# Last attention head: every tile transposed by DMA, half of one output product moved into the loop, and the first output loads split 16, 15 and 1 heads

## The chip, the cores and the metric

The kernel runs on one core of a Trainium2 chip. The metric is the device time of one execution in microseconds. The kernel before takes 1593.01 us, the median of three runs (1591.46 to 1596.07).

The engines named below are TensorE (PE; weight loads are listed as PEld), VectorE (DVE), ScalarE (ACT), GpSimd (POOL) and SyncE (SP), which here only issues DMAs. The DMAs that SP issues form one queue in program order: SP issues one, then waits for whatever the next one needs, then issues that. Each compute engine also runs its own instructions in program order.

## The reference

An adaptive layer norm block with attention over a cache, followed by a token mixer and an MLP:

```python
mod = (_silu(c) @ w_mod).reshape(c.shape[0], 6, 1, -1)
h = _layernorm(x) * (1 + ca) + sa
x = x + ga * _A_ref(h, A_k_cache, A_v_cache, A_wq, A_wo)
h = _layernorm(x) * (1 + cb) + sb
x = x + gb * _B_ref(h, B_w1, B_w2, B_w3, B_w4)

def _A_ref(x, k_cache, v_cache, wq, wo):      # Sq = 2048, D = 640, H = 32, Sk = 2048, Dh = 128
    q = (x @ wq) per head
    p = softmax(q @ k_cache^T * Dh ** -0.5)
    return (p @ v_cache, heads side by side) @ wo
```

`_B_ref` is layer norm, a product with w1, GELU, a shift of four groups of channels along the sequence, a product with w2, then layer norm, w3, GELU and w4. Inputs and output are bf16.

## The kernel before

**Tiles.** The 2048 queries are 16 tiles of 128 (`NQT`). Attention is a loop over 512 tiles (`NG` = 32 heads x 16 tiles), one step `s` for each, and 12 more steps that drain it (`PVD` = 8, `LAG` = 4). Below, "tile 3 of the last head" is step 496 + 3.

**One step.** For each half of the 2048 keys, PE writes scores to the two halves of `Sps` (`qk`, lines 294 and 15). DVE scales them into `negS` with a running minimum (line 584). POOL joins the two minima (594). ACT writes exp to the ring slot `Pb[s % 10]` (597). The probabilities must then be transposed, keys on the partitions, into `PTs[s % 10]`. PE multiplies them with V eight steps later (`pv`, line 307), ACT copies two tiles' results out (575), POOL divides by the row sum (455) and writes four tiles at a time to `o_scratch` in HBM (462).

**Two ways to transpose.** Of 16 tiles, 14 go through a DMA from the ring to the ring (`transpose`, line 230), in pairs where both neighbours go this way and singly otherwise. Tiles 3 and 10 (`PE_TILES`) go through PE instead: 16 transposes (`t_piece`, line 261) into the two PSUM banks `Oaug` and `QPp`, and a copy out of each (`t_evac`, by ACT, line 270, or by DVE, line 272). So a head has six pairs and two singles, tiles 2 and 11, in the DMA queue. The two banks are also used by the query projections of the next head (`q_piece`, line 245), of which the last head has none.

**The SP queue in a head.** Beside the transposes it holds the next head's K (line 213), wq (217) and V (222). In the last head these are absent. There, `load_ot` (505) begins to fetch attention outputs of the first two query tiles (a "pair", `pr` = 0, for all heads) from `o_scratch`, transposed, into `hTx`: heads 0 to 11 after tile 2, heads 12 to 23 after tile 9, heads 24 to 31 after the last tile. Behind these come `load_xt(0, 1)` (512), whose target covers the ring slots of the last tiles and which therefore waits until the last transpose has landed, and `load_ot(1)`, all 32 heads of query tiles 2 and 3, into `negS`.

**The wo product.** `a_pe(j)` (line 532) accumulates 32 heads for query tile j into one half of `Sps`, 640 columns as 512 + 128, two matmuls for a head. Tile 0 is done in parts: heads 0 to 11 at step 515, heads 12 to 23 at step 516, the rest after the loop. Tile 1 has heads 0 to 11 at step 518 and the rest after the loop. Tiles 2 to 15 follow whole. `a_s1` and `a_s2` (645 to 659) apply the gate, the residual and the second layer norm; then the mixer (`b_op` 707, `c_op` 772) and the MLP (`d_op` 787, `e_op` 836) follow.

The helper `Prog` (line 20) puts the waits in: every operation names what it reads and writes, and an engine waits on the last writer or the readers.

Of the kernel before, what the change touches and what calls it, by code (L numbers as in the profile page):

```python
# [8 lines left out]
BF16 = mybir.dt.bfloat16  # L9
F32 = mybir.dt.float32  # L10
# [113 lines left out]
def bass_adaLN_cond__mha_block_cached__mixer_s_mlp__prompt_kernel(  # L124
# [15 lines left out]
    NG = H * NQT  # L140
# [5 lines left out]
    with ExitStack() as es:  # L146
# [4 lines left out]
        mod_bc = sb("mod_bc", [128, 4 * D], F32)  # L151
        Sps = ps("Sps", [128, 2048], F32)
        PTp = ps("PTp", [128, 2048], BF16)
        Oaug = ps("Oaug", [128, 512], F32)
        QPp = ps("QPp", [128, 512], F32)
        QPb = QPp[:].bitcast(BF16)

        if True:
            with ExitStack() as es1:
# [44 lines left out]
                s_col = flat[:, CO + 7 * KT:CO + 8 * KT]  # L204
                assert CO + 8 * KT <= 2 * RP * SK and XO + NQT * D <= WO_ and WO_ + KT * 2 * D <= 10 * SK
                PO = PTp[:].bitcast(F32)
                JB = [Oaug[:, 0:512], QPp[:, 0:512]]
                JBb = [Oaug[:].bitcast(BF16), QPb]
                G = Prog(nc, es1, "a")

                def load_k(h):
# [11 lines left out]
                          ("v", hb), w=[("V", hb)])  # L223

                assert RP % 2 == 0 and NQT % 2 == 0
                is_pe = lambda g: g % NQT in PE_TILES

                def transpose(g, n):
                    b = g % RP
# [283 lines left out]
                        xt[:, 4 * c0:4 * c1], x2d[c0 * 512:c1 * 512, :].rearrange("(t p) d -> p t d", p=128)),  # L513
                        ("xt", c0), w=[("x1", t) for t in range(4 * c0, 4 * c1)] + ringk(XT0 + 4 * c0 * D, XT0 + 4 * c1 * D))

                OTC = [0, 12 * H // 32, 24 * H // 32, H]
                yn = [0]

                def ybank():
# [3 lines left out]
                def a_pe(j, b=None, parts=(0, 1, 2), hs=None):  # L523
                    if b is None:
                        b = ybank()
                    pr, z = divmod(j, 2)
                    h0, h1 = hs or (OTC[parts[0]], OTC[parts[-1] + 1])

                    def f(t):
                        for c0, cw in NC2:  # L530
                            for hh in range(h0, h1):
                                ins = t.matmul(YB[b][:, c0:c0 + cw], OTj[pr % 2][:, 2 * hh + z, :], wo[:, hh, c0:c0 + cw],  # L532
                                               start=(hh == 0), stop=(hh == H - 1))
                        return ins
                    G.op("tensor", f, r=[("OT", pr % 2, i) for i in parts] + ["wo"], w=[("S", b)])
                    return b

                YB = [Sps[:, 0:1024], Sps[:, 1024:2048]]
                LAG = 4
                for s in range(NG + PVD + LAG):  # L540
                    h, j = divmod(s, NQT)
                    g_ = s - PVD
                    evacs = []
                    if s <= 2:
                        for i in ((0,), (1, 2), range(3, len(MROW)))[s]:
                            mod_rows(i)
                    if s == 3:
                        G.op("gpsimd", lambda g: g.tensor_scalar(
                            out=mod_bc[:, 2 * D:3 * D], in0=mod_bc[:, 2 * D:3 * D], scalar1=1.0, scalar2=1.0, op0=ALU.add, op1=ALU.mult),
                            r=[("mod", i) for i in range(len(MROW))], w=["mod"])  # L550
                    for half in range(2):
                        if s < NG:
                            qk(s, half)
                        if half == 0 and s in (NG + PVD - 5, NG + PVD - 4):
                            b0 = a_pe(0, None if s == NG + PVD - 5 else b0, (s - NG - PVD + 5,))
                        if half == 0 and s == NG + PVD - 2:
                            b1 = a_pe(1, None, (0,))
                        if 0 <= g_ < NG:
                            pv(g_, half)
                        if s == 0 and half == 1:  # L560
                            q_head0(NQC - 1)
                        if h + 1 < H and 2 * j + half in QPIECE:
                            cc, q = QPIECE[2 * j + half]
                            q_piece(h + 1, cc, q)
                            if q == KT - 1:
                                evacs.append((q_evac, h + 1, cc))
                        for r in range(2):
                            g = s - 3 - r
                            if 0 <= g < NG and is_pe(g):
                                t_piece(g, r, half)  # L570
                                if half == 1:
                                    evacs.append((t_evac, g, r))
                    if 0 <= g_ < NG and g_ % 2 == 1:
                        p = g_ // 2
                        G.op("scalar", lambda a, p=p: a.copy(  # L575
                            Of[:, p % 4].rearrange("p z d -> p (z d)")[:, 0:259], PO[:, (p % 2) * 512:(p % 2) * 512 + 259]),
                            r=[("O", p % 2)], w=[("Of", p % 4)])
                    for fn, x, y in evacs:
                        if fn is q_evac or not by_dve(x, y):
                            fn(x, y)  # L580
                    for half in range(2):
                        if s < NG:
                            r8 = s % 8
                            G.op("vector", lambda v, half=half, s=s, r8=r8: v.tensor_scalar(  # L584
                                out=negS[:, s % 3, half * 1024:(half + 1) * 1024],
                                in0=Sps[:, half * 1024:(half + 1) * 1024],
                                scalar1=-SCALE, scalar2=None, op0=ALU.mult, op1=ALU.min,
                                accum_out=(nm0 if half == 0 else nm1)[:, r8:r8 + 1]),
                                r=[("S", half)], w=[("negS", s % 3), ("nmh", half, r8)])
                    for fn, x, y in evacs:  # L590
                        if fn is t_evac and by_dve(x, y):
                            fn(x, y)
                    if s < NG:
                        G.op("gpsimd", lambda g, r8=r8: g.tensor_scalar(  # L594
                            out=nm[:, r8:r8 + 1], in0=nm0[:, r8:r8 + 1], scalar1=nm1[:, r8:r8 + 1], scalar2=None, op0=ALU.min),
                            r=[("nmh", 0, r8), ("nmh", 1, r8)], w=[("nm", r8)])
                        G.op("scalar", lambda a, s=s, r8=r8: a.activation(  # L597
                            Pb[:, s % RP, :], negS[:, s % 3, :], ACT.Exp, bias=nm[:, r8:r8 + 1], scale=-1.0),
                            r=[("negS", s % 3), ("nm", r8)], w=[("Pb", s % RP)])
                        if not is_pe(s):  # L600
                            if s % 2 == 1 and not is_pe(s - 1):
                                transpose(s - 1, 2)
                            elif s % 2 == 1 or is_pe(s + 1):
                                transpose(s, 1)
                        if j == 2 and h >= 1 and h + 1 < H:
                            load_k(h + 1)
                        if h + 1 == H and j in (2, PVD + 1):
                            i = 0 if j == 2 else 1
                            load_ot(0, OTC[i], OTC[i + 1], i)
                        if j == 6 and h + 2 < H:  # L610
                            load_wq(h + 2)
                        if j == PVD + 1 and h + 1 < H:
                            load_v(h + 1)
                    if 0 <= s - PVD - LAG:
                        gr, z = divmod(s - PVD - LAG, 4)
                        if z == 0:
                            rcp(gr)
                        norm(gr, z)
                    if s == NG:
                        G.op("gpsimd", lambda g: g.memset(mhalf, -0.5), w=["mhalf"] + NEG)  # L620
                        load_ot(0, OTC[2], OTC[3], 2)
                        load_xt(0, 1)
                        load_ot(1)
                    if s == NG + 2:
                        load_xt(1, NQC)
# [16 lines left out]

                def a_s1(j, b):
                    u = j % 2
                    G.op("vector", lambda v: v.tensor_mul(out=tmp[:, u], in0=YB[b][:, 0:D], in1=mod_bc[:, 0:D]),  # L645
                         r=[("S", b), "mod"], w=[("tmp", u)] + (TMPK if j < 2 else []))
                    G.op("vector", lambda v: v.tensor_add(out=xt[:, j], in0=tmp[:, u], in1=xt[:, j]),
                         r=[("tmp", u)], w=[("x1", j)])
                    stats_of(0, j, xt[:, j], ("x1", j))
# [77 lines left out]

                for i in range(NQT):
                    if i < NQT - 2:
                        b = a_pe(0, b0, (2,)) if i == 0 else a_pe(1, b1, (1, 2)) if i == 1 else a_pe(i)  # L730
                        if i >= 3:
                            n_t(i - 3, i == 3)
                    if i == NQT - 3:
# [174 lines left out]
```

## Time and profile before

| what | us |
|---|---|
| median of three runs | 1593.01 |
| the profiled execution, its time | 1592.4 |
| its span in the trace | 1590.6 |
| PE busy in the span | 1477.4 |
| DVE busy | 1395.0 |
| ACT busy | 1295.8 |
| POOL busy | 622.0 |
| DMA share of the hardware queue, of 16 engines' span | 98.5% |

The 1.8 us between the profiled execution's time and its span lie outside the trace. Matmuls are pipelined, so a busy PE isn't PE at its peak. An `SPq` row is a DMA-issuing instruction: its duration is the time for which SP is held by the issue, and the data land some microseconds later. Idle time ahead of an instruction stands in brackets with what ended it.

### The profile page before, as it was taken

What the parts mean: (1) busy time and instruction counts of PE and PEld (TensorE: products, weight loads), DVE (VectorE), ACT (ScalarE), POOL (GpSimd) and SP (SyncE); (2) the same over time, 40 slices, a digit from 0 to 9 for tenths busy, and PEclk for the clock granted to TensorE, in tenths of its full rate; (3) what the DMA queues carried; (4) which work ended last, traced back from release to release, by engine and by line L of the source; (5) the groups of instructions that cost most, each with busy time, mean ns of one, the idle gap of its engine ahead of it and who ended that gap; (6) DMA issues with size and microseconds to landing.
All of it is one profiled execution on the core that took longest, in us unless ns stands there. A gap on an engine that the chain in (4) does not pass through costs nothing.

```text
span 1590.6 us, 33595 instructions
## 1 busy us (share of the span) xinstructions
PE 1477.4 (93%) x13976; PEld 916.9 (58%) x13207; DVE 1395.0 (88%) x2463; ACT 1295.8 (81%) x1145; POOL 622.0 (39%) x1396
## 2 busy tenths in 40 slices
PE   5899999999999999999999999999999889999999
PEld 3466655656565556665556565565656655555555
DVE  6999999999999999999999999999999646666435
ACT  4999999999999999999999999999999700036330
POOL 0244444444444444444444444444444523223100
PEclk9999999999999999999999999999999999999999
DMA  9999999999999999999999999999999997503000
GB/s 300 236 235 237 240 236 239 242 233 251 235 245 236 233 242 241 239 244 228 245 238 236 236 248 230 243 242 237 243 230 236 240 248 135 127 1 112 9 26 34
DMA packets 1167900, 333.53 MB, mean 210 GB/s; under 512 B 1148352, under 2 KB 1161728, under 8 KB 1167744
## 3 DMA queue, kind: packets, MB, share of 16 engines
q1 hardware_dynamic: 1161600, 314.59, 98.5%
q0 software_dynamic: 6144, 16.79, 3.7%
q8 instruction: 108, 1.77, 0.5%
q14 instruction: 48, 0.39, 0.1%
HBM read 43.48 MB, written 19.40 MB: 40 GB/s over the span
## 4 chain that ended last, share of the span: by engine, by line
DVE 34%; ACT 22%; PE 21%; DMA 13%; issue 9%; POOL 2%; SPq 0%; POOLq 0%; DVEq 0%
DVE negS L584 31%; ACT ring L597 18%; DMA ring<-ring 12%; PE Sps L532 8%; PE Sps L836 4%; ACT ring L270 2%; PE Oaug L787 2%; PE QPp L787 2%; PE Sps L772 1%; ACT kv L252 1%; ACT Of L575 1%; PE PTp L307 1%; DVE ring L272 1%; DMA negS<-o_scratch 1%; POOL small L594 1%
## 5 line engine op out<-in xcount | busy, mean ns | idle before, releaser
L584 DVE TENSOR_SCALAR_CACHE_REDUCE negS<-Sps 128x1024 f32<-128x1024 f32 x1024 | 1178.6, 1220 | 30.9 <-PE Sps L15 30.5
L597 ACT ACTIVATE ring<-negS,small 128x2048 bf16<-128x2048 f32 x512 | 1029.6, 2018 | 22.8 <-POOL small L594 20.7
L307 PEld LDWEIGHTS PTp<-kv,ring 128*128 128x128 bf16 x8192 | 550.7, 98 | 382.7 <-issue 112.9
L307 PE MATMUL PTp<-kv,ring 128*128 128x129 bf16 x8192 | 645.7, 220 | 49.0 <-DMA ring<-ring 48.6
L15 PE MATMUL Sps<-kv 128*128 128x512 bf16 x1024 | 387.9, 379 | 12.6 <-DVE negS L584 6.6
L594 POOL TENSOR_SCALAR small<-small 128x1 f32<-128x1 f32 x512 | 145.8, 285 | 631.5 <-DVE negS L584 631.5
L294 PE MATMUL Sps<-kv 128*128 128x512 bf16 x926 | 355.3, 384 | 21.9 <-DVE negS L584 10.8
L455 POOL TENSOR_SCALAR On<-Of,small 128x128 bf16<-128x128 f32 x512 | 190.0, 371 | 13.0
L294 PEld LDWEIGHTS Sps<-kv 128*128 128x128 bf16 x1024 | 98.3, 96 | 109.3 <-DVE negS L584 87.2
L448 POOL TENSOR_TENSOR small<-Of,small 128x4 f32<-128x4 f32 x128 | 133.1, 1040 | 9.2 <-ACT Of L575 9.2
L675 ACT COPY kv<-PTp 128x640 bf16<-128x640 bf16 x32 | 22.0, 692 | 127.7 <-PE PTp L672 127.6
L462 POOL DMA_DIRECT2D o_scratch<-On x128 | 103.1, 806 | 40.8 <-POOL On L455 37.2
L575 ACT COPY Of<-PTp 128x259 f32<-128x259 f32 x256 | 96.0, 375 | 14.3 <-PE PTp L307 14.3
L245 PE MATMUL Oaug<-hTx,kv 128*128 128x512 bf16 x264 | 100.4, 385 | 3.4 <-DVE hTx L404 3.4
L245 PE MATMUL QPp<-hTx,kv 128*128 128x512 bf16 x259 | 97.5, 381 | 2.4 <-ACT hTx L399 1.7
L584 DVE DVE_READ_ACCUMULATOR negS<-Sps 128x1 f32 x1024 | 84.9, 83 | 0.0
L631 POOL TENSOR_SCALAR negS<-negS 128x1 f32<-128x1 f32 x48 | 24.7, 514 | 138.5 <-DVE negS L640 138.3
L532 PE MATMUL Sps<-wo,negS 128*128 128x128 bf16 (+1 forms) x503 | 71.4, 300 | 4.5 <-DMA negS<-o_scratch 4.1
L532 PE MATMUL Sps<-wo,hTx 128*128 128x512 bf16 (+1 forms) x502 | 69.3, 297 | 0.5
L645 DVE TENSOR_TENSOR ring<-Sps,mod_bc 128x640 f32<-128x640 f32 x16 | 13.2, 825 | 62.1 <-PE Sps L532 40.7
L270 ACT COPY ring<-Oaug 128x1024 bf16<-128x1024 bf16 x64 | 65.4, 1022 | 0.0
L840 DVE TENSOR_TENSOR ring<-Sps,ring 128x640 f32<-128x640 f32 x15 | 12.4, 824 | 58.5 <-PE Sps L836 58.5
(91 smaller groups left out, 1043.4 us busy)
## 6 DMA issues: line engine op xcount, KB each, us to landing
kv<-in_A_v_cache_dram SPq DMA_DIRECT2D x32, 512.0 KB, 5.0
o_scratch<-On POOLq DMA_DIRECT2D x128, 128.0 KB, 3.8
kv<-in_A_wq_dram SPq DMA_DIRECT2D x32, 160.0 KB, 3.3
wo<-in_A_wo_dram SPq DMA_DIRECT2D x1, 5120.0 KB, 17.2
ring<-ring SPq DMA_TRANSPOSE x256, 7.0
ring<-in_A_x_dram SPq DMA_DIRECT2D x5, 640.0 KB, 7.0
ring<-in_w_mod_dram SPq DMA_DIRECT2D x1, 3200.0 KB, 13.3
out_dram<-wo SPq DMA_DIRECT2D x15, 160.0 KB, 1.8
```

Source lines behind the costliest of these rows:

```text
L15: return t.add_instruction(mybir.InstMatmult(name=t.bass.get_next_instruction_name(), ins=[t.lower_ap(rhs), t.lower_ap(lhsT)], outs=[t.low ...
L245: G.op("tensor", lambda t: t.matmul(JB[jb], wq[:, hb, q, :], hT[:, q, cc * 512:(cc + 1) * 512], start=(q == 0), stop=(q == KT - 1)), r=[(" ...
L294: ins = (t.matmul if c2 == 0 else partial(same_weights, t))(Sps[:, col:col + 512], QT[:, hb, j * 128:(j + 1) * 128], KTs[:, hb, col:col + ...
L307: ins = t.matmul(ob[:, 0:129], PTs[:, b, kt, :], Vaug[:, hb, kt, 0:129], start=(kt == 0), stop=(kt == NKT - 1))
L448: G.op("gpsimd", lambda g: g.tensor_tensor(out=rl[:, 4 * b:4 * b + 4], in0=Of[:].rearrange("p a z d -> p (a z) d")[:, 4 * b:4 * b + 4, 128 ...
L455: G.op("gpsimd", lambda g: g.tensor_scalar(out=On[:, b, z, :], in0=Of[:, 2 * b + z // 2, z % 2, 0:128], scalar1=rl[:, 4 * b + z:4 * b + z ...
L462: G.dma("gpsimd", lambda e: e.dma_start(o_scr[jj // 2:jj // 2 + 2, :, hh].rearrange("a p z d -> p a (z d)"), On[:, b].rearrange("p (a z) d ...
L532: ins = t.matmul(YB[b][:, c0:c0 + cw], OTj[pr % 2][:, 2 * hh + z, :], wo[:, hh, c0:c0 + cw], start=(hh == 0), stop=(hh == H - 1))
L575: G.op("scalar", lambda a, p=p: a.copy(Of[:, p % 4].rearrange("p z d -> p (z d)")[:, 0:259], PO[:, (p % 2) * 512:(p % 2) * 512 + 259]), r= ...
L584: G.op("vector", lambda v, half=half, s=s, r8=r8: v.tensor_scalar(out=negS[:, s % 3, half * 1024:(half + 1) * 1024], in0=Sps[:, half * 102 ...
L594: G.op("gpsimd", lambda g, r8=r8: g.tensor_scalar(out=nm[:, r8:r8 + 1], in0=nm0[:, r8:r8 + 1], scalar1=nm1[:, r8:r8 + 1], scalar2=None, op ...
L597: G.op("scalar", lambda a, s=s, r8=r8: a.activation(Pb[:, s % RP, :], negS[:, s % 3, :], ACT.Exp, bias=nm[:, r8:r8 + 1], scale=-1.0), r=[( ...
```

## The change

1. `is_pe` is false in the last head: its tiles 3 and 10 are transposed by DMA too, so the singles of tiles 2 and 11 become pairs.
2. `Oaug` and `QPp` become the two halves of one PSUM tensor `Jps`.
3. Tile 0's wo product accumulates in `Jps`. A new function `y0_pe` issues heads 0 to 15 one at a time in steps 501 to 511, each behind the scores of its half step, heads 16 to 30 in steps 512, 513 and 514, five each, and head 31 after the loop. `a_s1(0)` reads `Jps`.
4. Tile 1's wo product takes over the places of tile 0: heads 0 to 11 at step 515, 12 to 23 at 516, 24 to 30 at 518, head 31 after the loop.
5. `load_ot(0)` is cut into heads 0 to 15 (after tile 0's step, ahead of the pair of tiles 0 and 1), 16 to 30 (after tile 4's step, ahead of the pair of tiles 4 and 5) and head 31 (after the last tile).

```diff
-        Oaug = ps("Oaug", [128, 512], F32)
-        QPp = ps("QPp", [128, 512], F32)
-        QPb = QPp[:].bitcast(BF16)
+        Jps = ps("Jps", [128, 1024], F32)
...
-                JB = [Oaug[:, 0:512], QPp[:, 0:512]]
-                JBb = [Oaug[:].bitcast(BF16), QPb]
+                JB = [Jps[:, 0:512], Jps[:, 512:1024]]
+                JBb = [b.bitcast(BF16) for b in JB]
...
-                is_pe = lambda g: g % NQT in PE_TILES
+                is_pe = lambda g: g % NQT in PE_TILES and g < NG - NQT
...
-                OTC = [0, 12 * H // 32, 24 * H // 32, H]
+                OTC = [0, H // 2, H - 1, H]
...
+                def y0_pe(h0, h1, parts):
+                    def f(t):
+                        for c0, cw in NC2:
+                            for hh in range(h0, h1):
+                                ins = t.matmul(Jps[:, c0:c0 + cw], OTj[0][:, 2 * hh, :], wo[:, hh, c0:c0 + cw],
+                                               start=(hh == 0), stop=(hh == H - 1))
+                        return ins
+                    G.op("tensor", f, r=[("OT", 0, i) for i in parts] + ["wo"], w=[("J", 0), ("J", 1)])
+
+                W1 = [OTC[1] + (OTC[2] - OTC[1]) * i // 3 for i in range(4)]
+                Y0 = {}
+                u = NG - NQT + 5
+                for hh in range(OTC[1]):
+                    if hh % 3 == 0 and hh:
+                        u += 2
+                    Y0[(u + hh % 3 // 2, hh % 3 % 2) if hh % 3 < 2 else (u + 1, 0)] = (hh, hh + 1, (0,))
+                for i in range(3):
+                    Y0[(NG + i, 0)] = (W1[i], W1[i + 1], (1,))
...
-                        if half == 0 and s in (NG + PVD - 5, NG + PVD - 4):
-                            b0 = a_pe(0, None if s == NG + PVD - 5 else b0, (s - NG - PVD + 5,))
+                        if (s, half) in Y0:
+                            y0_pe(*Y0[s, half])
+                        if half == 0 and s == NG + PVD - 5:
+                            b1 = a_pe(1, None, (0,), (0, 12 * H // 32))
+                        if half == 0 and s == NG + PVD - 4:
+                            b1 = a_pe(1, b1, (0, 1), (12 * H // 32, 24 * H // 32))
                         if half == 0 and s == NG + PVD - 2:
-                            b1 = a_pe(1, None, (0,))
+                            b1 = a_pe(1, b1, (1,), (24 * H // 32, OTC[2]))
...
-                        if h + 1 == H and j in (2, PVD + 1):
-                            i = 0 if j == 2 else 1
+                        if h + 1 == H and j in (0, 4):
+                            i = 0 if j == 0 else 1
                             load_ot(0, OTC[i], OTC[i + 1], i)
...
-                    G.op("vector", lambda v: v.tensor_mul(out=tmp[:, u], in0=YB[b][:, 0:D], in1=mod_bc[:, 0:D]),
-                         r=[("S", b), "mod"], w=[("tmp", u)] + (TMPK if j < 2 else []))
+                    G.op("vector", lambda v: v.tensor_mul(out=tmp[:, u], in0=(YB[b] if j else Jps)[:, 0:D], in1=mod_bc[:, 0:D]),
+                         r=([("S", b)] if j else [("J", 0), ("J", 1)]) + ["mod"], w=[("tmp", u)] + (TMPK if j < 2 else []))
...
-                        b = a_pe(0, b0, (2,)) if i == 0 else a_pe(1, b1, (1, 2)) if i == 1 else a_pe(i)
+                        b = y0_pe(OTC[2], H, (2,)) if i == 0 else a_pe(1, b1, (2,)) if i == 1 else a_pe(i)
```

## The prediction

> **What bounds the kernel now.** I read the page first, for the engines and the DMA share, then the chain around the end of the loop, then the SP queue and ACT in order of time there, and last PE behind it. The page, parts 1 to 3:
>
> ```profile
> PE 1477.4 (93%) x13976; PEld 916.9 (58%) x13207; DVE 1395.0 (88%) x2463; ACT 1295.8 (81%) x1145; POOL 622.0 (39%) x1396
> DMA  9999999999999999999999999999999997503000
> q1 hardware_dynamic: 1161600, 314.59, 98.5%
> ```
>
> Four resources are nearly full, and DMA is full in every slice up to about 1310 us. The averages don't say which one sets the end of the loop. The chain of waits there, 1255 to 1310 us:
>
> ```profile
> 1259.15 1.86 ACT ring L597
> 1261.01 5.90 DMA ring<-ring
> ...
> 1268.31 7.50 DMA ring<-ring
> ...
> 1275.82 0.42 DMA ring<-in_A_x_dram
> 1276.25 13.54 DMA negS<-o_scratch
> 1289.79 0.45 issue
> 1290.23 9.79 PE Sps L532 x63
> ```
>
> PE starts query tile 2 of the wo product at 1290.23, when `load_ot(1)` has landed. The PE row of that moment carries its wait, and the stages behind it are full of PE (columns: stretch, length, PE, PEld, DVE, ACT, POOL busy, clock, DMA share, GB/s):
>
> ```profile
> 1290.23 18.49 PE L532 MATMUL Sps<-wo,negS 128*128 128x512 bf16 x126 [4.12 <-DMA negS<-o_scratch]
> 1310.00:1400.00 90.00, 89.47 (x683) 51.95 (x692) 59.79 (x111) 7.46 (x11) 29.06 (x42) 1.00 0.60 119
> 1400.00:1500.00 100.00, 99.03 (x645) 52.72 (x655) 58.87 (x119) 53.01 (x86) 25.65 (x48) 1.00 0.13 45
> ```
>
> So the end is 1290.23 plus some 300 us of PE work that the change leaves as it is. Tiles 0 and 1 of the wo product were already done 4.12 us earlier. The question is only when `load_ot(1)` lands. The SP queue ahead of it (start, time SP is held):
>
> ```profile
> 1233.12 7.08 SPq L230 DMA_TRANSPOSE ring<-ring  x2
> 1240.25 3.56 SPq L505 DMA_TRANSPOSE hTx<-o_scratch  x1
> 1243.85 13.49 SPq L230 DMA_TRANSPOSE ring<-ring  x3
> 1257.38 3.58 SPq L505 DMA_TRANSPOSE hTx<-o_scratch  x1
> 1261.01 11.65 SPq L230 DMA_TRANSPOSE ring<-ring  x3
> 1272.78 2.70 SPq L505 DMA_TRANSPOSE hTx<-o_scratch  x1
> 1275.82 0.38 SPq L512 DMA_DIRECT2D ring<-in_A_x_dram  x1
> 1276.25 11.56 SPq L505 DMA_TRANSPOSE negS<-o_scratch  x1
> ```
>
> The rows stand end to end; SP is never free. Its 8 transposes are the last head's: pair 0-1 and single 2; pairs 4-5, 6-7, 8-9; single 11 and pairs 12-13, 14-15. ACT in the same time, the last five exps (tiles 11 to 15) and the copies of tile 10 between them:
>
> ```profile
> 1250.86 2.00 ACT L597 ACTIVATE ring<-negS,small 128x2048 bf16<-128x2048 f32 x1
> 1253.17 2.00 ACT L597 ACTIVATE ring<-negS,small 128x2048 bf16<-128x2048 f32 x1 [0.30 <-POOL small L594]
> 1255.33 1.01 ACT L270 COPY ring<-Oaug 128x1024 bf16<-128x1024 bf16 x1
> 1256.24 2.01 ACT L597 ACTIVATE ring<-negS,small 128x2048 bf16<-128x2048 f32 x1
> 1258.14 1.01 ACT L270 COPY ring<-QPp 128x1024 bf16<-128x1024 bf16 x1
> 1259.03 2.02 ACT L597 ACTIVATE ring<-negS,small 128x2048 bf16<-128x2048 f32 x1
> 1261.19 2.02 ACT L597 ACTIVATE ring<-negS,small 128x2048 bf16<-128x2048 f32 x1
> ```
>
> Tile 11's exp ends at 1252.9 and its transpose is issued at 1261.01; tile 15's ends at 1263.2 and its pair goes at 1268.31. The queue is 5 to 8 us behind ACT. The chain's step from exp to DMA at 1261 is an inferred releaser; by the rows that transpose waited for SP, which was issuing heads 12 to 23. In the last head, work added to the DMA queue is paid for; work taken from ACT or PE is not.
>
> **The change part by part.**
>
> *Two more tiles in the queue (and the PE path gone).* PE loses 32 transposes (about 3.1 us), ACT three copies of 1.01, DVE one of 0.69: nothing, since the queue covers it. The queue gains two tiles, 2 x 0.52 MB. The single of tile 2 holds SP 2.71 us (part of the 7.08), that of tile 11 1.75. Six pairs hold it 7.08 - 2.71 + 13.49 + 11.65 - 1.75 = 27.76, 4.63 each. Two singles become pairs: 2 x 4.63 - 4.46 = +4.8. By tiles, 32.22 us for 14 is 2.30 each: +4.6. I take +4.6, the mean over more rows. Ends: +3.5 (two tiles at 1.75) and +6.5 (both pairs like the slowest here, 5.47).
>
> The Trainium skill (DMA: Bandwidth & Descriptors, Latency and other measured facts) gives DMA transposes 261 GB/s, and 350 to 400 where contiguous; the two tiles would then take 4.0 us, or 2.6 to 3.0, and by that estimate the sum below would be +5.4, or +4.0 to +4.4, which is within 0.3%, the absorbed rival's side. The rows move a 1.05 MB pair in 4.63 us, 227 GB/s, so the trace is below both.
>
> *Output loads 16, 15, 1.* 24 heads took 3.56 + 3.58 = 7.14 us, 0.30 each. 31 heads now stand ahead of the last transposes: 9.2, +2.1 (end +4.0, at the 0.36 a head of the 11.56 row). The last part shrinks from 2.70 to some 0.3, but SP doesn't get that back: `load_xt(0,1)` behind it waits for the last pair to land (1268.31 + 7.50 = 1275.81) and is issued at 1275.82. What comes back is that less data stand before `load_ot(1)`. That takes 13.54 to land; the four lone ones later take 11.3, 11.4, 10.3 and 9.9, mean 10.7, and the 0.64 MB of x at 239 GB/s make 2.7, or 13.4. The old part landed 1.6 us into it. So between 0 and 1.6 is returned; I take 0.8. The last pair may land sooner with little behind it (landings of the last head's transposes run from 5.2 to 8.5 us; 7.5 now): I take 0.3, ends 0 and 0.8.
>
> *Wo heads in the loop.* 12 heads took 3.42 us, 0.28 a head. With 1.45 heads a step, PE has 4 score matmuls (about 0.22 apart), 16 of PV (1.12) and 0.41: 2.41 against DVE's 2 x 1.14 = 2.29. The first piece stands behind the first scores of step 501, which were at 1232.8. It needs heads 0 to 15, now issued at 1233.12 for 4.75 us and landed some 2.6 behind that, 1240.5. PE, and through it DVE and ACT, stops for 7 us. PV and the second scores of that step stand behind. Exp of step 501 then ends about 1245.5 and that of 511 ten steps of 2.41 later, 1269.6. The queue reaches its pairs at 1251.4 (4.75 + two pairs + 4.45 from 1233.12) and 1274: it never runs dry, with over 4 us to spare. I take 0. Without that cover each us lost is an us at the end.
>
> *PE behind the loop.* From step 512, about 1267.5: 8 tiles of PV 9.0, 15 + 31 heads 12.9, two heads 0.6: done at 1290. The 28 heads taken away behind the loop (7.55 us) gain nothing: PE waits for `load_ot(1)` anyway.
>
> *Clock.* PE idled 4.12 us before 1290.23; the stretch 1290.2 to 1300.1 had a clock of 0.88, and its tile took 9.79 against 8.64 later: 1.15 lost. The idle time is now about 5.5. Loss between 0.7 and 2.4: I take +0.4, ends -0.5 and +1.3.
>
> The Trainium skill (TensorE: Matmul & The Clock Gate, What's actually happening) says that a free-running window of 3.4 us idle halves the clock and a busy one restores it, so that the loss depends on where the window falls; the drop to 0.88 after 4.12 us fits.
>
> *Sum:* 4.6 + 2.1 - 0.8 - 0.3 + 0.4 = **+6.0**. `load_ot(1)` lands at 1295.4. On the profiled execution (span 1590.6, 1592.4 with the 1.8 outside it) that is 1598.4. It lies 0.6 below the median of the runs, so against 1593.01 I say 1599.0, 0.38% slower.
>
> **The rivals.**
>
> *The queue absorbs it (no change).* If the added tiles cost the queue less (the 1.75 row) and the smaller part ahead of `load_ot(1)` gives all of its 1.6 back, the landing moves by 3.5 + 2.1 - 1.6 - 0.8 = 3.2 and the clock may give 0.5: +2.7, 1595.7. It could go down to PE's own 1290 plus the 0.3 of the last issue, 1593. For it: no K, wq or V in this head. Against: SP isn't free for a moment in it.
>
> *The loop runs dry.* If step 501 resumes over 4 us later than reckoned, or PE's steps take 2.8, the last exps come after the queue: +3 more, 1602. For it: nothing in the trace before has PE wait for an output load in the loop. Against: the 4 us to spare.
>
> *Faster.* The chain of waits is right and the exps, not the queue, set the last transposes. Then three ACT copies (3.0) go, the short last part returns 2.4 of SP, and PE, not stopped at 501, is ready at 1282: `load_ot(1)` lands 5 earlier, 1588. It decides as soon as SP waits for an exp in the last head. Against: 5 to 8 us of lag in the rows.
>
> **How the numbers follow.** Forecast 0.64, absorbed 0.14, dry 0.12, faster 0.10. About 0.3% (4.8 us, so 1597.8) is what a measurement of this kernel can tell from no change. The forecast's own range is 1595.5 (low ends) to 1603.5 (4.0 for the loads, 6.5 for the tiles, part of the rest), and 0.10 of its 0.64 lies under 1597.8. Slower: 0.54 + 0.12 = 0.66; same: 0.10 + 0.14 = 0.24; faster 0.10. The range 1592.5 to 1604.5 leaves out the faster case and the worst of the dry one, under 0.2.
>
> **What would show it.** Right: in the SP queue eight pairs end to end, the last ending near 1279; `load_ot(1)` issued near 1282 and landing near 1295; PE idle about 5 us before tile 2; a PE wait of some 7 us at the first `y0_pe`. Wrong: gaps in the SP queue inside the last head (dry), transposes issued right at the end of their exps (faster), or tile 2 starting before 1293 (absorbed).

## The result, and the profile after

The changed kernel takes 1600.03 us against 1593.91 for the kernel before, both medians of 17 runs of each. The ratio is 1.0042 with a 95% interval of 1.0030 to 1.0054, that is 6.7 us slower (4.8 to 8.6). The forecast was 1599.0, 0.38% slower.

The page of the changed kernel, parts 1 to 3, shows no engine in trouble. PE and ACT have the same shares as before and DVE 87% against 88%, and the hardware queue moved 1.04 MB more, which is the two tiles:

```profile
PE 1494.7 (93%) x14199; PEld 916.0 (57%) x13175; DVE 1394.1 (87%) x2462; ACT 1294.5 (81%) x1142; POOL 625.2 (39%) x1396
DMA  9999999999999999999999999999999995603000
q1 hardware_dynamic: 1165696, 315.63, 97.9%
```

The SP queue of the changed kernel, from the last head's first entry (start, time SP is held). The lines of the loads, the transposes and the wo product are two lower than in the kernel before; those of the loop's scaling and exp, which stand behind `y0_pe`, are 20 higher:

```profile
1234.57 4.65 SPq L503 DMA_TRANSPOSE hTx<-o_scratch  x1
1239.26 9.78 SPq L228 DMA_TRANSPOSE ring<-ring  x2
1249.16 4.57 SPq L503 DMA_TRANSPOSE hTx<-o_scratch  x1
1253.78 27.70 SPq L228 DMA_TRANSPOSE ring<-ring  x6
1281.58 1.19 SPq L503 DMA_TRANSPOSE hTx<-o_scratch  x1
1283.14 0.38 SPq L510 DMA_DIRECT2D ring<-in_A_x_dram  x1
1283.56 11.25 SPq L503 DMA_TRANSPOSE negS<-o_scratch  x1
```

The eight pairs stand end to end, as forecast. They take 9.78 + 27.70 = 37.48 us, 4.69 each. The issue of the last one ends at 1281.48, and the x load behind it goes out at 1283.14, when that pair has landed.

Two PE waits in order of time in the changed kernel (start, duration, and in brackets the idle time before and who ended it): the first `y0_pe`, and query tile 2 of the wo product:

```profile
1241.46 0.71 PE L540 MATMUL Jps<-wo,hTx 128*128 128x512 bf16 x2 [6.47 <-DMA hTx<-o_scratch]
1289.35 0.43 PE L530 MATMUL Sps<-wo,hTx 128*128 128x512 bf16 x2
1297.77 2.74 PE L530 MATMUL Sps<-wo,negS 128*128 128x512 bf16 x6 [7.99 <-DMA negS<-o_scratch]
```

And the chain of waits of the changed kernel there:

```profile
1283.56 14.16 DMA negS<-o_scratch
1297.72 0.05 issue
1297.77 2.31 PE Sps L530 x5
```

Tile 2 waits for `load_ot(1)`, as before. It starts at 1297.77 instead of 1290.23, 7.54 later, although PE had been done with tiles 0 and 1 for 8 us.

**How profiles are compared here.** Executions reach the last head at different times, though no edit here adds or takes a transfer ahead of it: the first entry of its SP queue (the pair of tiles 0 and 1 before, the 16 heads of the output load in the changed kernel) was issued at 1233.12 before, at 1234.57 in the changed kernel, and between 1229.2 and 1234.6 over all the profiled kernels below. So places are counted from that issue. By this count tile 2 starts at 1290.23 - 1233.12 = 57.1 before and at 1297.77 - 1234.57 = 63.2 after: 6.1 us, which lies inside the measured 4.8 to 8.6. From there to the end of the span it is 300.4 us before and 301.0 after.

### The profile page after: what moved, and what is told of

Same layout as the page of the kernel before. It is cut to its first block, busy times and chain, and to the rows that moved or that the text cites. A ratio compares the mean times of both kernels' runs of the same rounds, so it can differ in the third digit from the quotient of the medians.

```text
span 1598.8 us, 33783 instructions
## 1 busy us (share of the span) xinstructions
PE 1494.7 (93%) x14199; PEld 916.0 (57%) x13175; DVE 1394.1 (87%) x2462; ACT 1294.5 (81%) x1142; POOL 625.2 (39%) x1396
## 4 chain that ended last, share of the span: by engine, by line
DVE 31%; ACT 23%; PE 21%; DMA 14%; issue 8%; POOL 2%; SPq 0%; POOLq 0%
DVE negS L604 29%; ACT ring L617 19%; DMA ring<-ring 12%; PE Sps L530 8%; PE Jps L807 4%; PE Sps L856 4%; ACT ring L268 2%; PE Sps L792 1%; PE Jps L727 1%; ACT kv L250 1%; ACT Of L595 1%; PE PTp L305 1%; DMA negS<-o_scratch 1%; DVE ring L270 1%; POOL small L614 1%
## 5 line engine op out<-in xcount | busy, mean ns | idle before, releaser
L292 PE MATMUL Sps<-kv 128*128 128x512 bf16 x1024 | 393.5, 384 | 16.7 <-DVE negS L604 12.1
L15 PE MATMUL Sps<-kv 128*128 128x512 bf16 x1024 | 388.4, 379 | 0.0
L243 PE MATMUL Jps<-hTx,kv 128*128 128x512 bf16 x640 | 240.7, 380 | 7.0 <-ACT hTx L397 5.6
L259 PE MATMUL Jps<-ident,ring 128*128 128x128 bf16 x992 | 95.4, 218 | 0.0
L268 ACT COPY ring<-Jps 128x1024 bf16<-128x1024 bf16 x93 | 94.8, 1019 | 0.7 <-PE Jps L259 0.6
L250 ACT CAST kv<-Jps 128x512 bf16<-128x512 f32 x128 | 74.2, 580 | 5.8 <-PE Jps L243 5.6
L243 PEld LDWEIGHTS Jps<-hTx,kv 128*128 128x128 bf16 x640 | 62.7, 99 | 13.1 <-ACT hTx L397 6.0
L259 PEld LDWEIGHTS Jps<-ident,ring 128*128 128x128 bf16 x992 | 66.4, 97 | 1.0
```

What stands on the lines that cost most here:

```text
L15: return t.add_instruction(mybir.InstMatmult(name=t.bass.get_next_instruction_name(), ins=[t.lower_ap(rhs), t.lower_ap(lhsT)], outs=[t.low ...
L243: G.op("tensor", lambda t: t.matmul(JB[jb], wq[:, hb, q, :], hT[:, q, cc * 512:(cc + 1) * 512], start=(q == 0), stop=(q == KT - 1)), r=[(" ...
L259: ins = t.transpose(JBb[jb][:, z * 128:(z + 1) * 128], Pb[:, g % RP, kt * 128:(kt + 1) * 128], ident[:])
L268: G.op("scalar", lambda a: a.copy(dst, src), r=[("J", jb)], w=[("PT", g % RP, r)])
L292: ins = (t.matmul if c2 == 0 else partial(same_weights, t))(Sps[:, col:col + 512], QT[:, hb, j * 128:(j + 1) * 128], KTs[:, hb, col:col + ...
```

## The experiments

Theory, "the queue": what stands in the DMA queue of the last head, and what has to land behind it, sets when tile 2 can start; the two added tiles are the cost. Rival "the stop": PE's 6.5 us wait at the first `y0_pe`, and the halved clock behind it, delays the loop. Rival "the loads": the output loads put ahead of the transposes delay them. Each run was timed against the kernel before.

**The two tiles alone.**

```diff
-                is_pe = lambda g: g % NQT in PE_TILES
+                is_pe = lambda g: g % NQT in PE_TILES and g < NG - NQT
```

> The kernel before with one edit: the last head's tiles 3 and 10 go through DMA too, nothing else. Queue theory (the end is set by what stands in the DMA queue ahead of load_ot(1)): two tiles at 2.3 us each, +4.6 us against before, between +3.5 and +6.5; PE waits some 4 us longer before query tile 2 (8 to 9 against 4.1). Stop theory (the change is slower because PE stops at the first y0_pe, in the loop, and its clock halves there): no y0_pe here, so 0, within 1 us. Load theory (the earlier output loads are what costs): 0.

Measured: ratio 1.0040 (1.0023 to 1.0057), +6.4 us: all of the change's loss, with neither `y0_pe` nor the other loads. But the expected long wait for `load_ot(1)` isn't there. PE of this run:

```profile
1269.99 1.92 PE L307 MATMUL PTp<-kv,ring 128*128 128x129 bf16 x16 [5.90 <-DMA ring<-ring]
1288.12 7.55 PE L532 MATMUL Sps<-wo,hTx 128*128 128x512 bf16 x55
1295.72 4.48 PE L532 MATMUL Sps<-wo,negS 128*128 128x512 bf16 x20
```

PE waited 5.90 us for a late transpose, then worked through without another wait: tile 2 starts straight behind the 28 heads that this kernel keeps behind its loop. `load_ot(1)` landed at 1293.05, before that. Tile 2's place is 63.3 by the count above. So the late queue reaches tile 2 on two ways that are nearly equal: through `load_ot(1)`, and through the last tiles' product with V (PV) and the PE work behind it.

**The loads alone.**

```diff
-                OTC = [0, 12 * H // 32, 24 * H // 32, H]
+                OTC = [0, H // 2, H - 1, H]
...
-                        if h + 1 == H and j in (2, PVD + 1):
-                            i = 0 if j == 2 else 1
+                        if h + 1 == H and j in (0, 4):
+                            i = 0 if j == 0 else 1
```

> The kernel before with one edit: load_ot(0) cut into 16, 15 and 1 heads, issued after tile 0's and tile 4's step; tiles and wo products stay as they were (tile 0 takes 16 and 15 heads at steps 515 and 516, tile 1 takes 16 at step 518). Queue theory: the last pair is issued 2.1 us later, and 7 heads less stand ahead of load_ot(1), so the sum of bytes is unchanged: between 0 and +2, I take +1. Stop theory: 0. Load theory: the whole +6.

Measured: ratio 1.0001 (0.9988 to 1.0013). The rival "the loads" falls as the cause of the loss. The queue does show them: by the count above `load_ot(1)` goes out at 44.74 instead of 43.13, and tile 2 starts at 58.45 instead of 57.11. Tiles 2 and 3 then took 17.56 us instead of 18.49, since PE hadn't idled ahead of them. So the profile has some 0.4 us of loss left, which the timed runs can't tell from none.

PE stops in the loop of this run too. The pair of tiles 0 and 1 now stands behind 16 heads of loads, and their PV waits for it:

```profile
1243.10 1.05 PE L307 MATMUL PTp<-kv,ring 128*128 128x129 bf16 x8 [5.41 <-DMA ring<-ring]
```

In the 5 us behind this wait the granted clock is 0.66.

**The changed kernel with no wo heads in the loop.** Heads 0 to 20 of tile 0 all stand at step 512:

```diff
-                    Y0[(u + hh % 3 // 2, hh % 3 % 2) if hh % 3 < 2 else (u + 1, 0)] = (hh, hh + 1, (0,))
+                    pass
...
-                    Y0[(NG + i, 0)] = (W1[i], W1[i + 1], (1,))
+                    Y0[(NG + i, 0)] = (0 if i == 0 else W1[i], W1[i + 1], (0, 1))
```

> The changed kernel with heads 0 to 15 of tile 0's wo product moved from steps 501 to 511 to step 512, so that PE doesn't stop in the loop; the DMA queue is that of the changed kernel. Queue theory: as slow as the changed kernel, +5 to +7 us against before, with load_ot(1) landing at the same place. Stop theory: the 6 us come back, 0 against before. Load theory: +6.

Measured: ratio 1.0048 (1.0033 to 1.0063), as slow as the changed kernel. But against what was expected, the edit doesn't take the stop away. It moves it from `y0_pe` to the PV of tiles 0 and 1:

```profile
1244.65 1.05 PE L305 MATMUL PTp<-kv,ring 128*128 128x129 bf16 x8 [5.07 <-DMA ring<-ring]
```

So this run alone can't decide on "the stop". The rival falls by two others: the loads alone, above, stop PE for 5.41 us at the same place, and the next run for 4.86, and neither is measurably slower. What this run does show is the queue. `load_ot(1)` was issued at 1280.98, 48.5 us behind the head's first entry at 1232.46, against 49.0 in the changed kernel:

```profile
1232.46 4.53 SPq L503 DMA_TRANSPOSE hTx<-o_scratch  x1
1280.98 9.18 SPq L503 DMA_TRANSPOSE negS<-o_scratch  x1
```

And doing 16 heads inside the loop is worth nothing that can be measured: here they are all behind it.

**The changed kernel with the two tiles back on PE.** On top of the last edit:

```diff
-                is_pe = lambda g: g % NQT in PE_TILES and g < NG - NQT
+                is_pe = lambda g: g % NQT in PE_TILES
```

> The changed kernel with one part undone: the last head's tiles 3 and 10 go through PE again. Since both PSUM banks are then in use until step 511, heads 0 to 15 of tile 0's wo product stand at step 512, where they cost nothing in the run that moved them alone. Everything else of the change stays. Queue theory (the two tiles are the whole cost): as before, 0 within 1.5 us, 6 below the changed kernel. If the 16, 15, 1 split or the moved wo products cost anything that the two tiles hid: above before by that much.

Measured: ratio 1.0009 (0.9992 to 1.0026), no measurable difference from before (the interval leaves room for up to 4 us). With the tiles undone, the changed kernel's loss is gone; the rest of the change (banks, wo products, loads) shows neither a cost nor a gain. The stop is still there, with a granted clock of 0.59 in the 5 us behind it:

```profile
1245.53 1.05 PE L305 MATMUL PTp<-kv,ring 128*128 128x129 bf16 x8 [4.86 <-DMA ring<-ring]
```

**One tile, early or late.** The kernel before with tile 3 alone moved, and with tile 10 alone:

```diff
-                is_pe = lambda g: g % NQT in PE_TILES
+                is_pe = lambda g: g % NQT in PE_TILES and g != NG - NQT + 3
```

```diff
-                is_pe = lambda g: g % NQT in PE_TILES
+                is_pe = lambda g: g % NQT in PE_TILES and g != NG - NQT + 10
```

> The kernel before with only tile 3 of the last head moved from PE to DMA (tile 10 stays on PE). Both tiles together cost 6.4 us. Queue theory: half of it, +3 us (2 to 4). If what costs is a tile late in the head alone (the queue catches up on an early one): 0.

> The kernel before with only tile 10 of the last head moved from PE to DMA (tile 3 stays on PE). Queue theory: half of what both cost, +3 us (2 to 4), the same as for tile 3. If only the late tile costs: all of it, +6.

Measured: 1.0021 (1.0006 to 1.0037) for each, 3.3 us a tile. None, one, the other, both: 0, 3.3, 3.3, 6.4. It adds up within the intervals, which are wide (1 to 6 us for each single tile). The queue says the same more sharply. Places by the count above:

| kernel | `load_ot(1)` goes out | it lands | tile 2 starts |
|---|---|---|---|
| before | 43.13 | 56.67 | 57.11 |
| loads alone | 44.74 | 58.4 | 58.45 |
| tile 3 by DMA | 45.21 | 58.43 | 58.48 |
| tile 10 by DMA | 45.10 | 61.56 | 61.61 |
| both tiles by DMA | 47.05 | 60.65 | 63.32 |
| changed, tiles back on PE | 44.65 | 58.59 | 58.64 |
| changed, no wo heads in the loop | 48.52 | 62.24 | 62.52 |
| changed | 48.99 | 63.15 | 63.20 |

One tile delays the issue of `load_ot(1)` by 2.1 or 2.0 us, both by 3.9, the loads by 1.6, tiles and loads together by 5.4 to 5.9. The early tile costs the queue as much as the late one: it isn't made up for later. Behind the issue the profiles scatter. `load_ot(1)` took 13.2 us to land with tile 3 moved and 16.5 with tile 10 moved, and with tile 10 moved, alone or with tile 3, PE also waited over 5 us for a transpose at the end of the loop. How much of the 6.1 us at tile 2 is the loads' and not the tiles' can't be told from the timed runs: they give 6.4 (3.7 to 9.1) to the tiles alone.

**x behind `load_ot(1)`, in the kernel before.** An attempt at a gain:

```diff
-                        load_xt(0, 1)
                         load_ot(1)
+                        load_xt(0, 1)
```

> The kernel before with load_ot(1) issued ahead of load_xt(0,1). It then doesn't stand behind the wait for the last pair to land, and 0.64 MB of x no longer go before it. Queue theory: issued 0.7 us earlier and 2.7 us less of data ahead: 3.4 us faster than before, with PE's wait before query tile 2 going from 4.1 to below 1 us (PE itself is ready at 1286). If the end isn't set by the landing of load_ot(1): 0. If DVE then waits too long for x: some us slower.

Measured: ratio 1.0011 (0.9999 to 1.0024); no gain. `load_ot(1)` did land earlier, but a new wait took its place. DVE and PE of this run:

```profile
1289.02 0.82 DVE L645 TENSOR_TENSOR ring<-Sps,mod_bc 128x640 f32<-128x640 f32 x1 [29.59 <-DMA ring<-in_A_x_dram]
```

```profile
1290.38 9.83 PE L532 MATMUL Sps<-wo,negS 128*128 128x512 bf16 x59 [4.53 <-DVE ring L645]
```

In this kernel tile 2 uses the half of `Sps` that tile 0 leaves, so it waits for `a_s1(0)` to read it. And `a_s1(0)` writes to a part of the ring that shares a slot with the target of x, so it waits for x.

**The same in the changed kernel,** where tile 0 isn't in `Sps`:

> The changed kernel with load_ot(1) issued ahead of load_xt(0,1). Tile 2's wo product goes to a half of Sps that no a_s1 reads, so a late x doesn't hold it here as it did with the kernel before. Queue theory with the landing of load_ot(1) as the bound: 3 us faster than the changed kernel, so +3 against before, and PE's wait before tile 2 goes from 8 to about 5 us. If DVE again holds PE at tile 2 or 3: no gain, +6.

Measured: ratio 1.0061 (1.0039 to 1.0084): no gain. By the profile, `load_ot(1)` landed 1.8 us earlier by the count above (61.4 against 63.2), and the PE wait went from 7.99 to 6.37; but tiles 2 and 3 together then took 20.23 us against 19.17, at a lower clock (0.73 in the first 10 us, against 0.83). So the profile has 0.7 left of the gain. The timed runs have none, though their interval overlaps that of the changed kernel; whether anything else was lost stays open.

**Tiles on PE, and x late.** The changed kernel with tiles 3 and 10 back on PE, heads 0 to 20 at step 512, and `load_ot(1)` ahead of x:

> The changed kernel with tiles 3 and 10 through PE, heads 0 to 15 at step 512, and load_ot(1) ahead of load_xt(0,1). Queue theory: load_ot(1) lands some 3 us before its place in the kernel before; PE is ready at about the same time, so 2.5 us faster than before (0 to 3.5).

Measured: ratio 1.0000 (0.9981 to 1.0018). `load_ot(1)` landed at 1284.85, but PE was not ready:

```profile
1287.67 0.43 PE L530 MATMUL Sps<-wo,hTx 128*128 128x512 bf16 x2
1287.94 4.26 PE L530 MATMUL Sps<-wo,negS 128*128 128x512 bf16 x19
```

There is no wait left before tile 2. PE had lost 4.10 us earlier, at the PV of the pair of tiles 0 and 1, which now stands behind 16 heads of loads, and 1.88 at a later transpose.

**Three tiles on PE,** on top of that:

```diff
-                is_pe = lambda g: g % NQT in PE_TILES
+                is_pe = lambda g: g % NQT in (PE_TILES if g < NG - NQT else (3, 7, 11))
```

> As the last one, but three tiles of the last head (3, 7, 11) go through PE. Queue theory: one tile less, 2.3 us, in the queue; PE itself, ready at about 1286 to 1288, is then what tile 2 waits for: 2.5 to 4 us faster than before, with no wait for load_ot(1) ahead of tile 2. If ACT's two more copies make the last exps late: no more than the last one gains, or less.

Measured: ratio 1.0035 (1.0017 to 1.0054), slower. One tile less in the queue gained nothing; the way through PE has its own price at the end of the loop. PE of this run:

```profile
1270.62 7.44 PE L540 MATMUL Jps<-wo,hTx 128*128 128x512 bf16 x42 [3.65 <-ACT ring L268]
1296.79 0.43 PE L530 MATMUL Sps<-wo,hTx 128*128 128x512 bf16 x2
1297.06 2.32 PE L530 MATMUL Sps<-wo,negS 128*128 128x512 bf16 x10
```

The wo product of tile 0 waits for ACT to copy tile 11's transposes out of the same banks, and ACT does that copy among the last exps. From there PE has no wait and is at tile 2 only at 1297. So the rest of the time is PE's, and the queue isn't what ends last any more. Nor is the queue full here: SP stood free twice behind the second load, 3.1 us in all, and the last pair went 0.03 us after its exp:

```profile
1270.33 2.04 ACT L617 ACTIVATE ring<-negS,small 128x2048 bf16<-128x2048 f32 x1
1272.40 4.07 SPq L228 DMA_TRANSPOSE ring<-ring  x1
```

**A version meant to beat both.** The kernel before with its own loads, tile 0's wo product in `Jps` from step 512, and x late. Written as an edit of the changed kernel, with cuts:

```diff
-                is_pe = lambda g: g % NQT in PE_TILES and g < NG - NQT
+                is_pe = lambda g: g % NQT in PE_TILES
...
-                OTC = [0, H // 2, H - 1, H]
+                OTC = [0, 12 * H // 32, 24 * H // 32, H]
...
-                    Y0[(u + hh % 3 // 2, hh % 3 % 2) if hh % 3 < 2 else (u + 1, 0)] = (hh, hh + 1, (0,))
+                    pass
...
-                    Y0[(NG + i, 0)] = (W1[i], W1[i + 1], (1,))
+                    Y0[(NG + i, 0)] = (8 * i, 8 * i + 8, ((0,), (0, 1), (1,))[i])
...
-                        if half == 0 and s == NG + PVD - 2:
-                            b1 = a_pe(1, b1, (1,), (24 * H // 32, OTC[2]))
...
-                        if h + 1 == H and j in (0, 4):
-                            i = 0 if j == 0 else 1
+                        if h + 1 == H and j in (2, PVD + 1):
+                            i = 0 if j == 2 else 1
...
+                        load_ot(1)
                         load_xt(0, 1)
-                        load_ot(1)
```

> A version meant to beat both: the kernel before (tiles 3 and 10 through PE, loads of 12, 12 and 8 heads after tile 2, after tile 9 and after the last) with tile 0's wo product in the projections' banks from step 512 (8 heads a step, 8 after the loop), tile 1's in steps 515 and 516 and after the loop, and load_ot(1) ahead of load_xt(0,1). Queue theory: no stop of PE at step 504, load_ot(1) lands some 3 us earlier, PE is ready at about the same time: 2.5 us faster than before (0 to 3.5). If PE is the bound by then: 0.

Measured: ratio 1.0011 (0.9994 to 1.0028), no gain. By its profile tile 2 starts 55.8 us after the head's first entry (1231.26), 1.3 earlier than before:

```profile
1287.10 3.17 PE L530 MATMUL Sps<-wo,negS 128*128 128x512 bf16 x7 [3.58 <-DMA negS<-o_scratch]
```

But PE idled 3.58 us ahead of it, and tiles 2 and 3 took 20.18 us together against 18.5 before. The lower clock (0.73 from 1287 to 1297, against 0.88 in the first 9.9 us of tile 2 before) took back what the landing gave. No version tried here is measurably faster than the kernel before.

## Why the prediction was right

**The bound.** "The question is only when `load_ot(1)` lands": right for the kernel before and the changed one, whose tile 2 waits for it in both traces. It holds by less than the prediction thought: with the tiles alone, PE reached tile 2 by its own work at the same place, 2.7 us after `load_ot(1)` had landed.

**The chain's step from exp to DMA.** The prediction set it aside as an inferred releaser, since the queue lagged ACT by 5 to 8 us. The single tiles bear that out: added early or late, one delays the issue of `load_ot(1)` by the same 2.0 to 2.1 us.

**Two more tiles.** Reckoned +4.6 (3.5 to 6.5). In the profiles 14 tiles hold SP for 32.22 us before; 16 hold it for 37.48 in the changed kernel (+5.3), 36.93 with no wo heads in the loop (+4.7) and 35.98 with the tiles alone (+3.8). The term lies among these; which of the two ways of reckoning it is nearer isn't shown. The 6.4 us of the tiles alone are more than this term: in that profile `load_ot(1)` landed only 4.0 later, and the rest came on the way through PE, which the prediction didn't reckon with.

**Loads.** 31 heads ahead of the last transposes were reckoned at 9.2 us; the rows are 4.65 + 4.57 = 9.22. Less well judged was what comes back. From the end of the last pair's issue to the x load it was 3.16 us before and is 1.66: 1.5 returned, where I took 0.3 with an end of 0.8. `load_ot(1)` then took 14.16 to land instead of 13.54: -0.6, where I took +0.8. The two errors nearly cancel: +0.9 together against +1.1 reckoned. That is luck.

**Wo heads in the loop, the stop.** Reckoned: PE stops some 7 us at step 501, the queue never runs dry, cost 0. The stop is 6.47 us; the last exp ends at 1272.7 and its pair is issued at 1277.11, 4.4 us later (reckoned: over 4). ACT's last two rows in the loop:

```profile
1268.40 2.00 ACT L617 ACTIVATE ring<-negS,small 128x2048 bf16<-128x2048 f32 x1 [1.15 <-POOL small L614]
1270.69 2.00 ACT L617 ACTIVATE ring<-negS,small 128x2048 bf16<-128x2048 f32 x1
```

What the prediction missed is that the stop itself halves the clock: the granted clock of 1241.4 to 1246.5 is 0.51. It cost nothing here, since the 4 us of cover held. Nor is the stop the price of `y0_pe` alone: with no wo heads in the loop PE waited 5.07 us at nearly the same place, for the transposes of tiles 0 and 1.

**PE behind the loop.** Reckoned ready at 1290, 56.9 by the count; it was at 1289.8, which is 55.2. `load_ot(1)` was reckoned to land at 62.3 and landed at 63.15. So the wait was 7.99 instead of 5.5, from 1.7 on PE's side and 0.9 on the queue's.

**The sum.** From the head's first entry to tile 2: queue up to the last pair +7.4 (46.9 against 39.5; reckoned 6.7), returned 1.5, `load_ot(1)` 0.6 longer, last issue 0.4 shorter: +6.1. Then 0.7 to the end (reckoned +0.4 for the clock): 6.8, against +6.0 in the prediction and 6.7 (4.8 to 8.6) in the timed runs. The remaining 1.4 of the 8.2 us between the two spans was there before the last head began. Two sums of the prediction are a little off without weight: its low ends make 1595.7 and not 1595.5, and the queue's places in the loop 1251.6 and 1274.7 and not 1251.4 and 1274.

**The rivals.** "Absorbed" reckoned `load_ot(1)` 3.2 later; by the count it landed 6.5 later. "Dry" falls with the 4.4 us. "Faster" falls on its own condition: SP never waited for an exp in the last head.

## What to carry to other kernels

Here a queue that was held without a gap charged for every transfer added to it, wherever in the stretch it stood (2.0 to 2.1 us at `load_ot(1)` for one tile, 3.9 for two); time freed on engines that ran ahead of it was worth nothing. Read that from the queue's rows against the ends of the producers (here exp ends and issues, 5 us apart), not from the busy shares, and not from an inferred releaser in the chain. And when several chains end within some 4 us of each other, as here the landing, PE's own work and the exps, taking time from one of them moves the wait: five such attempts gained nothing that could be measured. Last, an edit meant to remove a wait may only move it: look for the wait in the experiment's own trace before its time is read.

## What was not expected of the hardware

Short waits of PE cost more than their length, and not in proportion to it. The wo product of tiles 2 and 3 takes 17.3 to 17.6 us together (the 17.3 is of a row that lacks two of the 128 matmuls) where PE had no wait ahead of it or one under 2 us. It took 18.9 after 2.87 us of idling (tile 3 alone), 19.0 after 3.56 (no wo heads in the loop), 20.2 after 3.58 (the version meant to beat both), 18.5 after 4.12 (before), 18.8 after 4.53 (x late in the kernel before), 20.2 after 6.37 (changed kernel with x late) and 19.2 after 7.99 (changed kernel). The stretches of the changed kernel at its two PE waits (stretch, length, PE, PEld, DVE, ACT, POOL busy, granted clock, DMA share, GB/s):

```profile
1241.40:1246.50 5.10, 5.04 (x27) 2.90 (x26) 1.55 (x3) 1.17 (x2) 0.65 (x2) 0.51 1.44 230
1297.70:1307.60 9.90, 9.83 (x56) 4.84 (x57) 1.98 (x4) 0.00 (x0) 0.74 (x2) 0.83 1.16 312
1307.60:1317.00 9.40, 9.40 (x81) 5.62 (x78) 5.97 (x12) 0.00 (x0) 2.89 (x4) 1.00 0.91 256
```

In the first stretch the clock is half. The second averages 0.83, because the clock is half for a part of it:

```profile
1294.24:1301.05 6.81, 3.28 (x8) 1.19 (x9) 1.58 (x4) 0.00 (x0) 1.69 (x3) 0.50 1.08 322
```

The same of the version meant to beat both, and of tile 3 alone:

```profile
1285.62:1292.43 6.81, 5.33 (x13) 1.90 (x14) 3.32 (x6) 0.00 (x0) 0.38 (x2) 0.50 0.73 218
1290.60:1294.00 3.40, 2.72 (x7) 1.04 (x8) 1.41 (x4) 0.00 (x0) 1.27 (x2) 0.50 1.03 339
```

The half clock lasts 6.8 or 3.4 us, with 1.00 on both sides, and it begins neither with the wait nor with its end. What PE loses is half of the part in which it works. Of the three, PE works 3.28, 5.33 and 2.72 us at half clock, which makes 1.6, 2.7 and 1.4 us; against the 17.56 of the undisturbed rows, tiles 2 and 3 took 1.6, 2.6 and 1.3 longer. So the place of the stretch decides as much as the length of the wait: a wait of 3.6 us cost 1.4 or 2.6 us more. The Trainium skill (TensorE: Matmul & The Clock Gate, What's actually happening) tells of a free-running activity window of 3413 ns, so that the moment at which the clock changes depends on where in it the first matmul falls. The stretches of 3.4 and 6.8 us agree with one and two such windows.

The DMA transposes from the ring to the ring moved a pair of 1.05 MB in 4.69 us, 224 GB/s, with nothing but themselves and the output loads in the queue. The Trainium skill (DMA: Bandwidth & Descriptors, Latency and other measured facts) has 261 GB/s for DMA transposes, measured on one kernel; the measurement decides here.
